# mLSTM cell and leaky-ReLU feed-forward: natural k of chunk 0 by transposing back, loads on other queues, another hand order of the first chunk

## The chip, the cores and the metric

The kernel runs on one core of one Trainium2 chip. The metric is device microseconds of one execution. A profile is one execution taken by the hardware profiler; its span runs from the first to the last instruction, and its own time is a little longer than the span.

The engines are TensorE (PE; its weight loads, PEld, are shown apart), VectorE (DVE), ScalarE (ACT), GpSimd (POOL) and SyncE (SP). SP and ACT both issue DMA transfers, each on a queue of its own; "SPq" and "ACTq" in the trace are such issues.

## The reference

Inputs are q, k, v and o_gate of shape (4 batches, 8 heads, 768 steps, 40), i_gate and f_gate of (4, 8, 768), and two weight matrices. The weights arrive as 64-bit floats.

```python
for t in range(S):
    m_new = np.maximum(f_gate[:, :, t] + m, i_gate[:, :, t])
    f_stab = np.exp(f_gate[:, :, t] + m - m_new)
    i_stab = np.exp(i_gate[:, :, t] - m_new)
    m = m_new
    C = f_stab * C + i_stab * einsum('bhd,bhe->bhde', vt, kt)
    n = f_stab * n + i_stab * kt
    h_tilde = einsum('bhde,bhe->bhd', C, qt)
    denom = np.maximum(np.abs(einsum('bhd,bhd->bh', n, qt)), 1.0)
    y[:, :, t] = sigmoid(o_gate[:, :, t]) * h_tilde / denom
x = y.transpose(0, 2, 1, 3).reshape(B * S, H * D)      # 3072 x 320
h = x @ w_in                                           # w_in 320 x 2048
out = np.maximum(0.01 * h, h) @ w_out                  # w_out 2048 x 320
```

## The kernel before

**Tiling.** Time is cut into six chunks of 128 steps. A step number s stands for one chunk and one batch: s = 4c + b. Within a chunk the recurrence is done in parallel form: scores of k against q, weighted by the gates, times v, plus the state that the chunk inherits. Chunk 0 inherits none, so it has code of its own. After a chunk of the cell come its feed-forward units, which `ff_units` returns as a list of small functions; the cell of chunk c and the feed-forward of chunk c-1 are interleaved.

**Who sets the order.** PE, DVE, ACT and POOL run in the order in which the program writes their instructions (`tc.manual_schedule`, line 1223). SP is not in that list: its issues are ordered by the framework. The DMA issues that the program gives to ACT stand in ACT's written order. Tiles in PSUM come from two rings of four buffers: tag "c" for the cell, tag "mm" for the feed-forward and the decay matrices.

**The first chunk** is `first_chunk` (line 1137), whose order is written out by hand. For each batch s from 0 to 3:

- `load` brings k and q (eight tokens of a head to a row) and v. `load_k` (391) brings k a second time, with a token on each partition ("natural"), 160 KB, into a slice of `rb_t`. `load_o` (396) brings the output gate, on ACT's queue.
- `u_transpose` (590) makes kqT, with the head dimension on the partitions, by matmuls against the identity, and copies it out of PSUM with an engine given to it: DVE for batches 0 and 1, ACT for 2 and 3.
- `spread_first` and `first_exp` (457, 486) make the decay matrix w of two batches at a time on PE, and its exponentials on ACT.
- `u_scores` (606) multiplies k and q and, on DVE, the decay matrix. `u_values` (690) multiplies by v, and `denominators` follows on DVE. `prep_o` is the tanh of the output gate on ACT. `gate` (698) makes x on DVE and POOL.
- `u_x` (786) transposes x on PE and copies it to xT with five ACT copies.
- `prep_vu` (508) scales v by the gates on POOL. `u_state` (680) multiplies natural k by it (`state`, 619) and copies the result into the state (`state_copy`, 630; two copies a batch, on DVE).

`narrow_weights` (244) turns a piece of the 64-bit weights into 32-bit in seven steps, an Abs on ACT and six on DVE; it is a generator, so the written order can put other work between two steps. `w_in` has four pieces, the first of which the feed-forward's units ffs[0] to ffs[3] need, the second ffs[4] to ffs[7]. ffs[0] and ffs[1] read x of batches 0 and 1, ffs[2] and ffs[3] of batches 2 and 3.

`gates(1)` (280) runs the scans of chunk 1 on DVE, `gates_exp(1)` (313) the exponentials on ACT, and writes a to the DRAM tensor `a_dr` (324). `spread` (438) reads it back, broadcast over partitions, as w of a step of chunk 1. `u_gates(1)` transposes the gates on PE and copies them with DVE.

After `first_chunk` the loads of chunk 1 are written (`feed`, 1115: v and the spread of w), and the main loop begins with ffs[2]; ahead of it in PE's order stands the first `u_split` (572) of chunk 1.

Of the kernel before, what the change touches and what calls it, by code (L numbers as in the profile page):

```python
# [19 lines left out]
def kernel(  # L20
# [28 lines left out]
    P = 128  # L49
# [41 lines left out]

    def load_fi(c):
        t = fi[c] = wk.tile([BH, 2, P], F32, name="fi")
        eng = nc.scalar if c < 3 else nc.sync
        eng.dma_start(t[:, 0, :], f_all[:, ts(c, P)])
        eng.dma_start(t[:, 1, :], i_all[:, ts(c, P)])

# [111 lines left out]
    def load_weights(n):  # L209

        m = n - QN
        if n < QN:
            dst = w_in[:, n, :]
        else:
            dst = w_out[:, 2 * m : 2 * m + 2, :].rearrange("p a d -> p (a d)")
        to = dst
        if wide:
            if n < 2:
                at = NF * GT - 2 * WC * (n + 1)
                raw = acts_l[:, at : at + 2 * WC].bitcast(U64)  # L220
            elif n < QN:
                raw = raw_t[:, WC * (n - 2) : WC * (n - 1)]
            elif m < 2:
                raw = w_out[:].rearrange("p f d -> p (f d)")[:, (2 + m) * WC : (3 + m) * WC].bitcast(U64)
            else:
                at = (4, 0, 1, 2, 3, 4)[m - 2] * HW
                raw = raw_t[:, at : at + HW]
            raws[n] = (raw, dst)
            to = raw
        if n < QN:  # L230
            src = moe_w_in[:, n * QC : (n + 1) * QC].rearrange("(k p) (r c) -> r p k c", p=DP, r=2)
            at = [0, 0]
# [80 lines left out]
    def gates_exp(c):  # L313
        bu, a, na = bus[c]
        if c == 0:
            nc.scalar.activation(bu[:, 1, :], i0[:BH], AF.Exp, bias=a[:BH, P - 1 :], scale=1.0)
            return
        for u in range(2):
            at = ts(u, SL)
            last = SL * (u + 1) - 1  # L320
            nc.scalar.activation(bu[:, 2, at], a[:, at], AF.Exp, bias=na[:] if u else 0.0, scale=1.0)
            nc.scalar.activation(bu[:, 1, at], bu[:, 0, at], AF.Exp, bias=a[:, last : last + 1], scale=1.0)
        if c > 0:
            nc.sync.dma_start(a_dr[c, 0].rearrange("u n t -> n u t"), a[:].rearrange("n (u t) -> n u t", u=2))
# [33 lines left out]
    def load(s):  # L358
        c, b = divmod(s, B)
        rows = ts(c, P)  # L360
        d = st.setdefault(s, {})
        n = s % NL
        d.update(k=kn[:, n], q=qn[:, n])
        if c == 0:
            d["va"] = S_t[n][:, 1]
            for t, src in ((kn, k), (qn, q)):
                nc.sync.dma_start(  # L367
                    t[:, n].rearrange("p h d -> p (h d)")[:, : TJ * D], src[b, :, rows, :].rearrange("h (g j) d -> h g (j d)", j=TJ),
                )
# [18 lines left out]
        if s < B + 2:  # L388
            load_late(s, 1)

    def load_k(s):
        to = rb_t[s % NR][:, 0, s // NR * Dm : (s // NR + 1) * Dm].rearrange("p (h d) -> p h d", d=D)
        nc.sync.dma_start(to, k[s, :, :P, :].rearrange("h p d -> p h d"))
        st[s]["k"] = to

    def load_o(s):
        c, b = divmod(s, B)
        at = NF * GT - 4 * WC - (s + 1) * Dm
        st.setdefault(s, {})["o"] = acts_l[:, at : at + Dm]
        nc.scalar.dma_start(  # L400
            st[s]["o"].rearrange("p (h d) -> p h d", d=D), o_gate[b, :, ts(c, P), :].rearrange("h p d -> p h d"),
        )

# [31 lines left out]

        return blocks(rb_t[s % NR][:, i, QW : QW + RL])[:, :, :w]

    def spread(s):

        c, b = divmod(s, B)  # L440
        d = st[s]
        w = wk.tile([P, H, P], F32, name="w", bufs=NL)
        d["w"] = w[:].rearrange("p h t -> p (h t)")[:, : H * SL].rearrange("p (h t) -> p h t", t=SL)
        for u in range(2):
            nc.sync.dma_start(d["w"][ts(u, SL)], a_dr[c, 0, u, b * H : (b + 1) * H, :].partition_broadcast(SL))

    def spread_q(s):

# [157 lines left out]
    def u_scores(s):  # L606
# [9 lines left out]
        for r in range(2):  # L616
            nc.vector.tensor_tensor(w[:, r::2, :], w[:, r::2, :], sc[r][:], op=ALU.mult)

    def state(s):
        c, b = divmod(s, B)  # L620
        d = st[s]
        dC = d["dC"] = psc.tile([P, PR, 2, V1], F32, name="dC", tag="c")
        for h in range(H):
            rows = slice(DP * (h % 2), DP * (h % 2) + D)
            nc.tensor.matmul(
                dC[rows, h // 2].rearrange("p k d -> p (k d)"), lhsT=d["k"][:, h, :D],
                rhs=d["vu"][:, h].rearrange("p k d -> p (k d)"), start=True, stop=True,
            )

    def state_copy(s):  # L630
        for r in range(2):
            rows = slice(DP * r, DP * r + D)
            nc.vector.tensor_copy(S_v[s % NL][SL : SL + D, 0, r::2, :, :V1], st[s]["dC"][rows])

    def state_of(s, u):

# [477 lines left out]

    def feed(s):
        load(s)
        spread(s)

    def feed_slowly(s):

# [16 lines left out]
    def first_chunk():  # L1137

        for n in range(2):
            load(n)  # L1140
        load_o(0)
        load_o(1)
        load_fi(1)
        load_weights(0)
        for n in range(2, B):
            load(n)
        load_weights(1)
        for n in range(B):
            load_k(n)
# [8 lines left out]
        u_transpose(1, nc.vector.tensor_copy)  # L1158
        load_kq(B)
        load_kq(B + 1)  # L1160
        load_weights(2)
        u_scores(0)
        u_scores(1)
        prep_o(0)
        prep_o(1)
        w = narrow_weights(0)
        next(w, None)
        load_o(2)
        load_o(3)
        load_fi(2)  # L1170
        ab = spread_first(a, 2)
        first_exp(ab, 2)
        prepare_tiles()
        next(w, None)
        next(w, None)
        u_values(0)
        gate(0)
        u_values(1)
        gate(1)
        prep_vu(0)  # L1180
        prep_vu(1)
        prepare_step(0)
        prepare_step(1)
        u_transpose(2, nc.scalar.copy)
        u_transpose(3, nc.scalar.copy)
        u_x(0)
        u_x(1)
        for _ in w:
            pass
        ffs = ff_units(0)  # L1190
        u_scores(2)
        u_scores(3)
        gates(1)
        gates_exp(1)
        ffs[0]()
        w = narrow_weights(1)
        next(w, None)
        prep_o(2)
        prep_o(3)
        next(w, None)  # L1200
        u_values(2)
        gate(2)
        next(w, None)
        u_values(3)
        gate(3)
        ffs[1]()
        u_x(2)
        for _ in w:
            pass
        u_x(3)  # L1210
        u_state(0)
        u_state(1)
        prep_vu(2)
        prep_vu(3)
        u_gates(1)
        u_state(2)
        u_state(3)
        prepare_step(2)
        prepare_step(3)
        return ffs  # L1220
# [123 lines left out]
```

## Time and profile before

| | |
|---|---|
| median of 3 runs | 514.63 us (513.19 to 515.49) |
| the profiled execution, its own time | 512.01 us |
| its span | 510.2 us |
| mean granted TensorE clock | 0.983 |
| PE busy | 493.4 us, 97% of the span |
| DVE, ACT, POOL busy | 338.6, 172.9, 144.2 us |
| DMA moved | 59.90 MB |

The page cuts the span into 40 slices of 12.8 us and gives, for each, the busy share of an engine in tenths (9 is 90% or more), the granted clock of TensorE in tenths, and the busy share of the DMA engines. A row of the timeline reads: start, duration, engine, line, operation, output<-input, shape, count, and in brackets the idle time ahead of it with what ended it. A row of the waits reads: the engine and line that waited, the one waited for, then microseconds in total, how often, and the longest.

### The profile page before, as it was taken

To read this page: it belongs to the slowest core of one execution; us is meant where nothing else is said; L and a number is where in the kernel's file an instruction comes from. 1 tells how busy PE (TensorE), PEld (TensorE's weight loads), DVE (VectorE), ACT (ScalarE), POOL (GpSimd) and SP (SyncE) were. 2 spreads that over 40 slices of the span, in tenths; PEclk is the share of its full clock that TensorE was granted. 3 is DMA by queue.
4 is the path that set the end of the run, shared out by engine and by line. 5 is a ranking of instruction groups with operands and counts; after the bars stand their busy time and mean duration, and the time that the engine had idled before them with its cause. 6 is when DMAs were issued, how large, how long until landed. Compare 5 with 4: busy or idle time off the path is not lost.

```text
span 510.2 us, 13235 instructions
## 1 busy us (share of the span) xinstructions
PE 493.4 (97%) x5346; PEld 384.4 (75%) x5346; DVE 338.6 (66%) x553; ACT 172.9 (34%) x462; POOL 144.2 (28%) x177
## 2 busy tenths in 40 slices
PE   8959798999999999999999999999999999999997
PEld 6848687867755469965479965489955489999997
DVE  4556999899973976924976734866623767864831
ACT  3163666752452331042421143511322510035210
POOL 3161725424320501620502701403700302200011
PEclk9878899999999999999999999999999999999999
DMA  6999886886460584872684772784861211200001
GB/s 140 184 161 174 175 221 152 217 159 149 90 165 9 114 165 120 151 155 90 138 164 122 144 163 77 156 155 111 167 176 33 58 53 39 89 5 1 1 1 51
DMA packets 161836, 59.90 MB, mean 117 GB/s; under 512 B 124336, under 2 KB 152560, under 8 KB 161776
## 3 DMA queue, kind: packets, MB, share of 16 engines
q1 hardware_dynamic: 117488, 51.20, 44.0%
q10 hardware_dynamic: 44288, 7.87, 9.6%
q8 instruction: 42, 0.69, 0.6%
q14 instruction: 18, 0.15, 0.1%
HBM read 52.33 MB, written 6.70 MB: 116 GB/s over the span
## 4 chain that ended last, share of the span: by engine, by line
PE 83%; SPq 5%; DMA 5%; DVE 2%; ACT 2%; POOL 2%; issue 1%; POOLq 0%; ACTq 0%; DVEq 0%
PE ph L813 32%; PE po L891 30%; PE pq L998 6%; PE po L848 6%; PE pT L748 3%; PE sd L667 3%; DMA acts<-in_moe_w_in_dram 2%; SPq L367 1%; DMA qn<-in_q_dram 1%; SPq L235 1%; PE sd L672 1%; DMA raw<-in_moe_w_in_dram 1%; PE tk L582 1%; PE hN L718 1%; SPq L414 1%
## 5 line engine op out<-in xcount | busy, mean ns | idle before, releaser
L813 PE MATMUL ph<-xT,w_in 64*128 64x512 f32 (+1 forms) x960 | 180.3, 527 | 0.0
L813 PEld LDWEIGHTS ph<-xT,w_in 64*128 64x128 f32 x960 | 92.5, 190 | 73.9 <-issue 68.0
L891 PEld LDWEIGHTS po<-w_out,acts 128*128 128x128 f32 x640 | 87.3, 190 | 3.4 <-issue 3.0
L891 PE MATMUL po<-w_out,acts 128*128 128x160 f32 x640 | 89.1, 300 | 0.0
L821 ACT ACTIVATE acts<-ph 128x512 f32<-128x512 f32 (+1 forms) x96 | 45.1, 522 | 119.7 <-PE ph L813 107.0
L645 POOL TENSOR_TENSOR S<-S,f 40x336 f32<-40x336 f32 x36 | 31.1, 863 | 130.9 <-PE pT L748 96.0
L677 DVE TENSOR_TENSOR qn<-w,sd 64x512 f32<-64x512 f32 x40 | 27.4, 684 | 41.5 <-PE sd L672 28.9
L506 ACT ACTIVATE w<-w,gT 128x64 f32<-128x64 f32 x160 | 41.2, 337 | 22.7 <-DMA S<-in_v_dram 11.2
L891 PE MATMUL po<-raw,acts 128*128 128x160 f32 x320 | 44.7, 300 | 0.0
L891 PEld LDWEIGHTS po<-raw,acts 128*128 128x128 f32 x320 | 43.6, 190 | 0.3
L848 PE MATMUL po<-w_out,acts 128*128 128x320 f32 x128 | 36.5, 437 | 0.0
L498 POOL TENSOR_TENSOR w<-w,i 128x512 f32<-128x512 f32 x20 | 28.4, 1429 | 24.4 <-DMA w<-a_dr 14.6
L762 POOL TENSOR_TENSOR xb<-xb,den 128x320 f32<-128x320 f32 x16 | 11.6, 727 | 76.9 <-DVE xb L759 76.9
L755 DVE STREAM_TRANSPOSE hb<-pT 128x512 f32<-128x512 f32 x16 | 11.4, 713 | 31.0 <-PE pT L748 30.8
L848 PEld LDWEIGHTS po<-w_out,acts 128*128 128x128 f32 x128 | 23.6, 190 | 9.3 <-issue 0.3
L559 DVE TENSOR_TENSOR qn<-kqT,ea 64x512 f32<-64x512 f32 x32 | 27.5, 860 | 1.0
L926 POOL TENSOR_TENSOR y<-y,raw 128x160 f32<-128x160 f32 x10 | 8.9, 894 | 64.2 <-ACT y L925 64.2
L667 PEld LDWEIGHTS sd<-kqT 40*64 40x64 f32 x640 | 20.0, 135 | 6.1 <-issue 6.1
L766 DVE STREAM_TRANSPOSE x<-xb 128x512 f32<-128x512 f32 x16 | 18.0, 1128 | 7.7 <-POOL xb L762 7.7
L891 PE MATMUL po<-raw 128*128 128x160 f32 x160 | 22.5, 299 | 0.0
L891 PEld LDWEIGHTS po<-raw 128*128 128x128 f32 x160 | 22.0, 190 | 0.0
L667 PE MATMUL sd<-kqT 40*64 40x64 f32 x640 | 21.6, 220 | 0.0
(185 smaller groups left out, 698.4 us busy)
## 6 DMA issues: line engine op xcount, KB each, us to landing
rb<-in_k_dram SPq DMA_DIRECT2D x64, 80.0 KB
rb<-in_q_dram SPq DMA_DIRECT2D x64, 80.0 KB
rb<-in_o_gate_dram SPq DMA_DIRECT2D x64, 80.0 KB
ea<-a_dr SPq DMA_DIRECT2D x32, 128.0 KB
raw<-in_moe_w_out_dram SPq DMA_DIRECT2D x6, 640.0 KB
w<-a_dr ACTq DMA_DIRECT2D x24, 128.0 KB
xT<-x_dr SPq DMA_DIRECT2D x32, 96.0 KB
x_dr<-x SPq DMA_DIRECT2D x64, 40.0 KB
```

Source lines behind the costliest of these rows:

```text
L498: nc.gpsimd.tensor_tensor(w, w, cm2.unsqueeze(1).to_broadcast([P, H, SL]), op=ALU.add)
L506: yield nc.scalar.activation(w[:, h, :], w[:, h, :], AF.Exp, bias=gT[c][:, 0, bh : bh + 1], scale=1.0)
L559: nc.vector.tensor_tensor(mixed(s)[rows, 1 - r], d["kqT"][rows, 1].rearrange("p (h t) -> p h t", t=SL), d["ea"][rows], op=ALU.mult,)
L645: nc.gpsimd.tensor_tensor(new, old, g, op=ALU.mult)
L667: nc.tensor.matmul(bank[1 - u][toks, h, :], lhsT=kqT[rows, 0, ts(h, SL)], rhs=kqT[rows, 1, ts(h, SL)], start=True, stop=True,)
L677: nc.vector.tensor_tensor(mixed(s)[toks, u], w[toks], bank[1 - u][toks], op=ALU.mult)
L766: nc.vector.transpose(in_blocks(xq[:]), xb[:].rearrange("p (j n) d -> p j n d", n=TB))
L813: nc.tensor.matmul(ph[r][:, cols], lhsT=w_row(r, slot, j), rhs=xT[DP * r : DP * (r + 1), slot, cols], start=(slot == 0), stop=(slot == KC ...
L821: nc.scalar.activation(acts[:, f, cols], ph[r][:, cols], AF.Prelu, alpha=0.01)
L848: nc.tensor.matmul(po[n][:], lhsT=acts[:, f, ts(n, P)], rhs=w_out[:, f, :], start=(f == 0), stop=(f == NF - 1),)
L891: nc.tensor.matmul(bank[:], lhsT=left[:, f, :], rhs=right[:, f, :], start=f == 0, stop=f == KH - 1)
L998: nc.tensor.matmul(bank[r][:, e, :], lhsT=left(r)[rows, e], rhs=right(r)[rows], start=n == 0, stop=n == len(terms) - 1,)
```

## The change

- `load_k` is removed. A new `u_natural` makes natural k of chunk 0 by transposing kqT back on PE, four 128x128 transposes per batch, with one ACT copy into the same place.
- The o loads of batches 2 and 3 are issued by SP, right after the loads of q, k and v; those of batches 0 and 1 stay on ACT. The f and i gates of chunk 2 are issued by SP.
- The write of a to `a_dr` for chunk 1 is issued by ACT, and so are the spreads of w for the first two steps of chunk 1 (4 and 5), which now stand in `first_chunk`.
- The two copies of kqT of batch 1 and all state copies of chunk 0 run on ACT.
- The hand order of `first_chunk` is another. Loads of k and q of step 5 stand behind w_in's third piece.

```diff
     def load_fi(c):
-        eng = nc.scalar if c < 3 else nc.sync
+        eng = nc.scalar if c < 2 else nc.sync
...
         if c > 0:
-            nc.sync.dma_start(a_dr[c, 0].rearrange("u n t -> n u t"), a[:].rearrange("n (u t) -> n u t", u=2))
+            eng = nc.scalar if c == 1 else nc.sync
+            eng.dma_start(a_dr[c, 0].rearrange("u n t -> n u t"), a[:].rearrange("n (u t) -> n u t", u=2))
...
-    def load_k(s):
-        to = rb_t[s % NR][:, 0, s // NR * Dm : (s // NR + 1) * Dm].rearrange("p (h d) -> p h d", d=D)
-        nc.sync.dma_start(to, k[s, :, :P, :].rearrange("h p d -> p h d"))
-        st[s]["k"] = to
-
-    def load_o(s):
+    def load_o(s, eng):
...
-        nc.scalar.dma_start(
+        eng.dma_start(
...
-    def spread(s):
+    def spread(s, eng):
...
-            nc.sync.dma_start(d["w"][ts(u, SL)], a_dr[c, 0, u, b * H : (b + 1) * H, :].partition_broadcast(SL))
+            eng.dma_start(d["w"][ts(u, SL)], a_dr[c, 0, u, b * H : (b + 1) * H, :].partition_broadcast(SL))
...
+    def u_natural(s):
+
+        nk = psc.tile([P, PR, P], F32, name="nk", tag="c")
+        for j in range(PR):
+            nc.tensor.transpose(nk[:, j], st[s]["kqT"][:, 0, ts(j, P)], ident[:])
+        to = rb_t[s % NR][:, 0, s // NR * Dm : (s // NR + 1) * Dm].rearrange("p (h d) -> p h d", d=D)
+        nc.scalar.copy(to, nk[:].rearrange("p j (r d) -> p (j r) d", r=2)[:, :, :D])
+        st[s]["k"] = to
...
     def state_copy(s):
...
-            nc.vector.tensor_copy(S_v[s % NL][SL : SL + D, 0, r::2, :, :V1], st[s]["dC"][rows])
+            nc.scalar.copy(S_v[s % NL][SL : SL + D, 0, r::2, :, :V1], st[s]["dC"][rows])
...
     def feed(s):
         load(s)
-        spread(s)
+        if "w" not in st[s]:
+            spread(s, nc.sync)
```

The body of `first_chunk` after the change, from the loads on:

```python
load(0); load(1); load_o(0, nc.scalar); load_o(1, nc.scalar); load_fi(1)
load_weights(0); load(2); load(3); load_o(2, nc.sync); load_o(3, nc.sync); load_weights(1)
gates(0); gates_exp(0); warm(9); ab = spread_first(a, 0); gates_T(0, bu); first_exp(ab, 0)
u_transpose(0, nc.vector.tensor_copy); u_transpose(1, nc.scalar.copy)
prep_vu(0); prep_vu(1)
load_kq(B); load_fi(2); load_weights(2); load_kq(B + 1)
u_scores(0); ab = spread_first(a, 2); u_scores(1)
prep_o(0); prep_o(1); u_natural(0); u_natural(1)
u_values(0); gate(0); u_values(1); gate(1)
first_exp(ab, 2); prepare_tiles()
w = narrow_weights(0); next(w, None)
u_x(0); u_x(1)
u_transpose(2, nc.scalar.copy); u_transpose(3, nc.scalar.copy)
for _ in w: pass
ffs = ff_units(0)
u_state(0); u_state(1); prepare_step(0); prepare_step(1)
u_scores(2); ffs[0](); u_scores(3)
u_values(2); prep_o(2); gate(2); u_values(3); prep_o(3); gate(3)
gates(1); gates_exp(1); ffs[1]()
w = narrow_weights(1); next(w, None); next(w, None)
u_x(2); u_x(3); prep_vu(2); prep_vu(3)
for _ in w: pass
u_gates(1)
for n in (B, B + 1): st[n] = {}; spread(n, nc.scalar)
u_natural(2); u_state(2); u_natural(3); u_state(3)
prepare_step(2); prepare_step(3)
```

More of the change, by code (lines that the diff above doesn't have):

```diff
@@ L1140, in first_chunk @@
             load(n)
-        load_o(0)
-        load_o(1)
+        load_o(0, nc.scalar)
+        load_o(1, nc.scalar)
         load_fi(1)
@@ L1146, in first_chunk @@
             load(n)
+        load_o(2, nc.sync)
+        load_o(3, nc.sync)
         load_weights(1)
-        for n in range(B):
-            load_k(n)
         gates(0)
@@ L1157, in first_chunk @@
         u_transpose(0, nc.vector.tensor_copy)
-        u_transpose(1, nc.vector.tensor_copy)
+        u_transpose(1, nc.scalar.copy)
+        prep_vu(0)
+        prep_vu(1)
         load_kq(B)
+        load_fi(2)
+        load_weights(2)
         load_kq(B + 1)
-        load_weights(2)
         u_scores(0)
+        ab = spread_first(a, 2)
         u_scores(1)
@@ L1165, in first_chunk @@
         prep_o(1)
[L1166 to L1175, printed above, removed]
+        u_natural(0)
+        u_natural(1)
         u_values(0)
@@ L1179, in first_chunk @@
         gate(1)
[L1180 to L1183, printed above, removed]
+        first_exp(ab, 2)
+        prepare_tiles()
+        w = narrow_weights(0)
+        next(w, None)
+        u_x(0)
+        u_x(1)
         u_transpose(2, nc.scalar.copy)
         u_transpose(3, nc.scalar.copy)
-        u_x(0)
-        u_x(1)
         for _ in w:
@@ L1190, in first_chunk @@
         ffs = ff_units(0)
+        u_state(0)
+        u_state(1)
+        prepare_step(0)
+        prepare_step(1)
         u_scores(2)
+        ffs[0]()
         u_scores(3)
+        u_values(2)
+        prep_o(2)
+        gate(2)
+        u_values(3)
+        prep_o(3)
+        gate(3)
         gates(1)
         gates_exp(1)
-        ffs[0]()
+        ffs[1]()
         w = narrow_weights(1)
[L1197 to L1206, printed above, removed]
+        for _ in range(2):
+            next(w, None)
         u_x(2)
+        u_x(3)
+        prep_vu(2)
+        prep_vu(3)
         for _ in w:
             pass
[L1210 to L1214, printed above, removed]
         u_gates(1)
+        for n in (B, B + 1):
+            st[n] = {}
+            spread(n, nc.scalar)
+        u_natural(2)
         u_state(2)
+        u_natural(3)
         u_state(3)
```

## The prediction

> **What bounds the kernel now.** I read the page's slices first, then the windows by stage, and then only the stage that is not full of TensorE work.
>
> ```profile
> PE   8959798999999999999999999999999999999997
> PEclk9878899999999999999999999999999999999999
> DMA  6999886886460584872684772784861211200001
> ```
>
> From the sixth slice on TensorE is busy and at full clock. The holes and the low clock lie in the first 60 us, and there the transfers are dense. The windows say it in microseconds (columns: length, then busy time of PE, weight loads, DVE, ACT, POOL; granted clock, DMA share, GB/s).
>
> ```profile
> 30.00:36.00 6.00, 2.85 (x10) 1.74 (x12) 1.32 (x1) 5.99 (x13) 4.06 (x8) 0.75 0.96 134
> 54.00:60.00 6.00, 3.89 (x98) 3.33 (x100) 5.74 (x13) 2.03 (x3) 4.65 (x11) 0.74 0.90 175
> 60.00:140.00 80.00, 78.00 (x1106) 62.39 (x1103) 74.75 (x108) 45.96 (x125) 33.00 (x30) 1.00 0.72 163
> 140.00:500.00 360.00, 360.00 (x3514) 274.47 (x3513) 225.52 (x367) 102.62 (x282) 86.69 (x101) 1.00 0.45 100
> ```
>
> After 60 us TensorE has 2.0 us of idle in 440. So the time of the whole kernel is the moment at which TensorE reaches the third feed-forward unit, ffs[2], plus a tail that the diff does not touch. In the trace that moment is 59.46. Every microsecond by which it moves is a microsecond of the kernel.
>
> What holds it up before that? The waits of the first 60 us, and the timeline of ScalarE and TensorE:
>
> ```profile
> PE xt L795 <- ACT kqT L604: 4.9, 1, 4.9
> PE dC L625 <- POOL vu L520: 2.5, 2, 2.2
> ACT w L491 <- DMA acts<-in_o_gate_dram: 7.8, 1, 7.8
> SPq L393 <- DMA acts<-in_moe_w_in_dram: 9.0, 3, 5.8
> ```
>
> ```profile
> 22.09 2.70 ACTq L400 DMA_DIRECT2D acts<-in_o_gate_dram  x2
> 26.20 2.82 ACTq L95 DMA_DIRECT2D fi<-in_f_gate_dram  x1
> 29.07 0.43 ACTq L96 DMA_DIRECT2D fi<-in_i_gate_dram  x1
> 29.55 2.32 ACT L491 ACTIVATE w<-ab 128x256 f32<-128x256 f32 x8 [7.79 <-DMA acts<-in_o_gate_dram]
> 31.67 3.93 ACT L604 COPY kqT<-tkq 128x512 f32<-128x512 f32 x4
> ...
> 32.98 0.66 PE L795 MATMUL xt<-ident,x 128*128 128x128 f32 x2 [4.88 <-ACT kqT L604]
> ...
> 50.24 0.44 PE L795 MATMUL xt<-ident,x 128*128 128x128 f32 x2
> 50.52 0.27 PE L796 MATMUL xt<-ident,x 128*64 128x128 f32 x1
> ...
> 59.46 2.79 PE L813 MATMUL ph<-xT,w_in 64*128 64x256 f32 x20
> ```
>
> ScalarE computes nothing from 21.75 to 29.55: it stands at four DMA issues. Behind them wait its exponentials, the copies of the transposes, and so TensorE.
>
> **How an issue waits.** The trace's completion records (the last of the 16 increments of a transfer's semaphore) explain those issues. The second o load goes out at 24.39; the transfer eight places ahead of it, counted over both queues together, completed at 24.37. The f load goes out at 26.20, after one that completed at 26.18. The k loads go out at 29.67, 31.26 and 33.62, after w_in pieces that completed at 29.65, 31.24 and 33.60. None of these issues needs the data it waited for. In this kernel an issue needs a place that the transfer eight ahead has given up, whichever engine issued either of them, and an engine that reaches it early stands still.
>
> **The change, part by part.** I rebuilt the order of the four engines by hand up to ffs[2], each instruction at its traced duration, each started when its engine, its inputs and its PSUM buffer (four in rotation) are free. Done so for the kernel before, the sum puts ffs[2] at 60.0 against 59.46 in the trace; 0.6 comes off the new sum too.
>
> 1. *The four loads of natural k (L393) go.* Nothing waits for them: they complete at 36.36 to 38.98, and their first reader runs at 52.0. What they free is the stream: 640 KB, about 0.9 us per load by the spacing of these completions, 3.5 us in all for everything behind.
>
> 2. *In their place 16 transposes and four copies.* A 128x128 transpose costs 0.14 us at full clock (L795 at 50.24, its follower 0.28 later, two of them) and 0.22 at half (32.98). So 2.2 to 3.6 us on TensorE: 1.2 ahead of values(0), on the path, the rest in a hole. A copy of 128x320 from PSUM is not in the trace; L798 takes 0.37 for 128x256, L542 0.46 for 128x320 from SBUF. I take 0.44, four times, on ScalarE.
>
> 3. *The o and f/i issues go to SyncE.* ScalarE is free at 21.75 instead of 29.50: 7.8 us. On SP they queue ahead of w_in(1), which completes at 35.3 and is not read before 44.8: that costs nothing unless SP falls 9 us behind.
>
> 4. *More on ScalarE.* The two copies of kqT(1) fall into idle time at 12 to 15. Eight state copies come over from DVE (0.33 each there; 64-row copies on ScalarE are 0.26 to 0.37, I take 0.31: 2.5 us). The first exponentials of batches 2 and 3 stand ahead of the Abs of w_in(0), which ends at 24.2 instead of 21.75; DVE's six steps on it end at 32.9.
>
> 5. *The hand order.* From there: u_x(1) 27.6, its five copies until 29.4 (1.64), four kqT copies at 0.98 until 33.3, scores(2) 34.5, ffs[0] until 36.8 (2.3; before it ran at 40.30 to 44.2), scores(3) 1.2 and two times values at 1.85 until 41.7, ffs[1] until 43.9 (before 50.2). DVE: gate(3) 42.7, gates(1) 1.7, exponentials 1.0: 45.4. So far the change gains 6 us.
>
> 6. *What is left stands in one row on ScalarE.* From 45.4: the issue of a_dr 0.5, Prelu 0.6, Abs of w_in(1) 1.4, ten copies of xT 3.3, four spread issues at 0.57 = 2.3, copy of natural k(2) 0.45, state(2) on TensorE 0.5, its copy 0.6, natural k(3) 0.45, state(3) 0.5, u_split 1.1. TensorE, done with u_gates at 46.3, waits for this row about 8 us. ffs[2]: 57.4, less 0.6 = 56.8. Four of the six microseconds are lost again, and without any DMA wait the change gains **2.7 us**.
>
> 7. *The wait.* a_dr now stands in ScalarE's row. SyncE's order is not written by hand, and before, a_dr went out late:
>
> ```profile
> 50.99 0.54 SPq L324 DMA_DIRECT2D a_dr<-a  x1
> 55.67 1.13 SPq L445 DMA_DIRECT2D w<-a_dr  x2
> ```
>
> Its data was ready at 43.2; four v loads, an o load and two pieces of w_in(3) went first, and the transfer eight ahead completed at 50.05. On SyncE that cost nothing. On ScalarE everything in point 6 is behind it, and DVE's steps on w_in(1) after the Abs. Bounds: with the same neighbours, the eighth ahead is now the q load of batch 5 (it has moved behind w_in(2)); by the stream 3.5 us earlier it completes near 47.0, a wait of 1.6. Were a_dr put behind all that SyncE can issue without chunk 1's gates, it would be a v load of batch 5 (61.49 before; less 3.5, less 1.5 for the spreads that no longer stand ahead): 56.5, a wait of 11.1. Below that, nothing: 0. In the order of before a_dr was already placed 7 us of transfers behind its data; now the hand order puts the gates behind ffs[0], both values and both gates, while SyncE's list is four loads shorter, so its place moves back, not forward. I take 52, the middle: a wait of **6.6 us**. The four spreads then find their places free.
>
> Sum: -2.7 + 6.6 = +3.9. It is made on the profiled execution (512.01, span 510.2) and carried to the median: 514.63 + 3.9 = **518.5**.
>
> Two rules of the Trainium skill, beside the rows. "DMA: Bandwidth & Descriptors", section "Issuing engines are not separate DMA queues", says that the issuing engine changes nothing but the sequencer's issue time. By it alone a_dr and the spreads would cost ScalarE their 2.8 us of issue and no wait, 511.9; the issues at 24.39 and 26.20 show a wait besides. "TensorE: Matmul & The Clock Gate", Part 4, gives some 275 ns for a 128x128 transpose in a kernel and says that transposes don't count as activity for the clock; an estimate from it is 4.4 us instead of 2.2 to 3.6, and a stretch at half clock after natural(0) and (1), up to 1.7 us. The rows at 50.24 speak against the first; for the second no row here has transposes alone.
>
> **Rivals.** *No wait (chance 0.24).* a_dr finds its place free because SyncE is far behind in issuing. For it: from 36 to 45 SP's issues follow each other at 0.6 us without waiting. Against: all four ScalarE issues in the dense stretch waited or were long. Time 514.6 - 2.7 = 511.9; if the 1.3 us of waits behind POOL at 82 to 84 go too, 510.6. *A small wait eats the gain (0.26).* Between 0.2 and 5 us, the lower bound above among it: 512.1 to 517; at a wait of 2.7, 514.6. That the removed loads were hidden anyway belongs here: by themselves they give nothing. *The wait decides (0.50).* From 5.3 us of wait the kernel is slower by over 0.5%, up to 11.1 - 2.7 = +8.4: 523.0.
>
> **Numbers.** About 0.5% (2.6 us) is what a measurement of this kernel can tell from no change. The forecast is the third case, 518.5, its own range 517.2 to 523.0. The range over all is 510.6 to 523.0: from the gain without waits to the longest wait. Faster 0.24, same 0.26, slower 0.50, the cases as they stand.
>
> **What would show it.** In the changed profile: L491 for batches 2 and 3 near 21 and ffs[0] near 34.5 (points 3 to 5); a TensorE hole ahead of L625 for batch 2, ended by the natural copy; ScalarE idle ahead of L324's issue, with the wait put to a load it does not read. If that issue follows the exponentials within 1 us, the forecast is wrong and the first rival right. If ffs[0] isn't there before 38, my order by hand is wrong.

## The result and the profile after

The changed kernel takes 523.16 us (median of 4 runs, 522.65 to 523.75), the kernel before 515.06 on the same chip: ratio 1.016, interval 1.0125 to 1.0196. It is slower by 8.1 us. The forecast was slower by 3.9, with 523.0 as the upper end of its range.

The profiled execution of the changed kernel took 523.52 us, its span is 521.7: 11.5 us more than the span of before. The medians differ by less, because the profiled execution of before, 512.01, lies 3.0 below the median of its runs. Moments below are from the profiles, gains and losses from the medians.

The page's slices of the changed kernel (13 us each) show where it went:

```profile
PE   7887079999999999999999999999999999999997
PEclk9978579999999999999999999999999999999999
DMA  7899975854344086595295674484871311200001
```

The fifth slice, 52 to 65 us, holds no TensorE work at all; before, it was seven tenths full. The windows put it in microseconds (columns as before: length, busy PE, weight loads, DVE, ACT, POOL, granted clock, DMA share, GB/s):

```profile
48.00:54.00 6.00, 2.10 (x10) 1.63 (x10) 0.00 (x0) 0.33 (x2) 1.42 (x4) 0.56 1.07 223
54.00:60.00 6.00, 0.00 (x0) 0.00 (x0) 2.73 (x3) 4.63 (x12) 0.00 (x0) 0.50 0.95 261
60.00:66.00 6.00, 0.00 (x0) 0.00 (x0) 4.53 (x6) 0.40 (x2) 0.00 (x0) 0.50 1.13 223
60.00:140.00 80.00, 70.61 (x1156) 57.95 (x1157) 65.10 (x96) 44.20 (x113) 28.29 (x26) 0.92 0.61 134
```

In the first of these windows ScalarE and VectorE stand nearly still as well, in the third ScalarE; the transfers alone are dense throughout. From 60 to 140 TensorE is busy for 70.61 us (78.00 before); 8.4 of the 9.4 us that it is idle lie before 72.7. The timeline of the changed kernel (start, length, engine, line; a "q" marks the issue of a transfer) names the instructions:

```profile
47.28 0.26 ACT L321 ACTIVATE bu<-a 32x64 f32<-32x64 f32 x1 [7.26 <-DVE a L295]
54.89 0.34 ACTq L325 DMA_DIRECT2D a_dr<-a  x1
55.27 0.66 ACT L826 ACTIVATE acts<-ph 128x256 f32<-128x256 f32 x2 [6.95 <-DMA raw<-in_moe_w_in_dram]
61.25 5.89 ACTq L441 DMA_DIRECT2D w<-a_dr  x4
67.19 0.43 ACT L621 COPY rb<-nk 128x320 f32<-128x320 f32 x1 [6.78 <-DMA w<-a_dr]
67.75 0.79 PE L630 MATMUL dC<-vu,rb 128*40 128x42 f32 x16 [17.28 <-ACT rb L621]
72.71 2.65 PE L818 MATMUL ph<-xT,w_in 64*128 64x256 f32 x22
```

Read it from the bottom. ffs[2] starts at 72.71; before, at 59.46. TensorE had waited 17.28 us for the copy of natural k of batch 2. That copy stood behind four spreads on ScalarE, whose issues took from 61.25 to 67.14. These stood behind ten copies and the Abs, and those behind the write of a_dr, which went out at 54.89, though its data was there at 47.3 (VectorE's L295) and ScalarE was through the exponentials ahead of it at 48.3. The releaser in brackets at L826, a piece of w_in, is nothing that the Prelu reads: it is the transfer whose place the write took.

The completion records of the semaphores, read as in the prediction, confirm each wait:

| issue on ScalarE | goes out | the transfer eight ahead is complete |
|---|---|---|
| write of a_dr | 54.89 | 54.868 (a piece of w_in(3)) |
| spread 1 | 61.25 | 61.232 (w_out) |
| spread 2 | 63.16 | 63.135 (w_out) |
| spread 3 | 65.31 | 65.289 (a v load) |
| spread 4 | 66.69 | 66.669 (a v load) |

All five went out within 0.03 us of the completion of a transfer they have nothing to do with. What a "place" is can be read from the issues' records: in every run the transfers that SyncE and ScalarE issue share eight semaphores, handed out in turn, and an issue goes out after the transfer before it on its own semaphore has completed.

### The profile page after: what moved, and what is told of

Its sections match the earlier page's. It is cut to its first block, busy times and chain, and to the rows that moved or that the text cites. A ratio compares the mean times of both kernels' runs of the same rounds, so it can differ in the third digit from the quotient of the medians.

```text
span 521.7 us, 13262 instructions
## 1 busy us (share of the span) xinstructions
PE 491.7 (94%) x5362; PEld 384.0 (74%) x5362; DVE 330.2 (63%) x543; ACT 179.4 (34%) x476; POOL 138.4 (27%) x177
## 4 chain that ended last, share of the span: by engine, by line
PE 79%; SPq 7%; DMA 5%; DVE 4%; ACT 2%; POOL 1%; issue 1%; ACTq 0%; POOLq 0%
PE po L896 30%; PE ph L818 29%; PE pq L1003 6%; PE po L853 5%; PE pT L753 3%; DMA S<-in_v_dram 3%; PE sd L672 3%; SPq L377 3%; SPq L235 2%; DMA w<-a_dr 1%; DMA qn<-in_q_dram 1%; SPq L410 1%; PE sd L677 1%; SPq L95 1%; DVE raw L269 1%
## 5 line engine op out<-in xcount | busy, mean ns | idle before, releaser
L818 PE MATMUL ph<-xT,w_in 64*128 64x512 f32 (+1 forms) x960 | 178.5, 523 | 0.0
L818 PEld LDWEIGHTS ph<-xT,w_in 64*128 64x128 f32 x960 | 91.2, 187 | 73.1 <-issue 67.9
L826 ACT ACTIVATE acts<-ph 128x512 f32<-128x512 f32 (+1 forms) x96 | 45.2, 522 | 126.6 <-PE ph L818 106.8
L760 DVE STREAM_TRANSPOSE hb<-pT 128x512 f32<-128x512 f32 x16 | 11.5, 717 | 30.9 <-PE pT L753 30.8
```

Source lines behind the costliest of these rows:

```text
L818: nc.tensor.matmul(ph[r][:, cols], lhsT=w_row(r, slot, j), rhs=xT[DP * r : DP * (r + 1), slot, cols], start=(slot == 0), stop=(slot == KC ...
L826: nc.scalar.activation(acts[:, f, cols], ph[r][:, cols], AF.Prelu, alpha=0.01)
```

## The experiments

Each run stands beside runs of the kernel before on its own chip (medians 513.4 to 515.1); ratios are to those, and 0.1% is 0.5 us. Two variants from different chips are better compared by their ratios than by their medians. "ffs[2]" is its start in the run's profile.

### Where the five issues of the gates stand

**All five on SyncE, the rest of the change kept.**

```diff
-            eng = nc.scalar if c == 1 else nc.sync
-            eng.dma_start(a_dr[c, 0] ...)
+            nc.sync.dma_start(a_dr[c, 0] ...)
...
-        for n in (B, B + 1): st[n] = {}; spread(n, nc.scalar)
```

> The changed kernel with chunk 1's write of a to a_dr and the four spreads of steps 4 and 5 issued by SyncE again, as before; all else of the change stays. Theory (ScalarE stands at DMA issues that need a place given up by a transfer eight ahead): the 6.6 us at the write and the 4.5 us between the spreads go, and the spreads' own 2.3 us too; ffs[2] comes at 57 to 60 instead of 72.7, 509 to 513 us. Rival (the new hand order and the copies moved to ScalarE cost the time; the DMA waits only fill a hole that is there anyway): ffs[2] stays above 66, 519 us or more.

Measured: 517.31 us, ratio 1.0069 (1.005 to 1.0088); ffs[2] at 58.80. The theory of the wait is right for ffs[2], which comes 13.9 us earlier, and the time was wrong: only 5.9 us of that arrive (4.7 by the ratios). The timeline of this run shows what took the rest:

```profile
67.37 0.82 ACT L501 ACTIVATE w<-w,gT 128x64 f32<-128x64 f32 x3 [5.89 <-POOL w L493]
...
68.65 4.68 PE L817 MATMUL ph<-xT,w_in 64*128 64x256 f32 x20 [5.03 <-ACT acts L825]
```

There is a second gate. The exponentials of step 4 (L501) stand ahead of the Prelus of ffs[2] on ScalarE. They need GpSimd's mask of w, and w needs the spreads, which land at 64.2 to 66.8. So the third unit waits 5.03 us. Behind that hole it runs almost wholly at half clock (until 72.98), 4.68 us for 20 matmuls where the two units ahead took 4.82 for 40: some 2.3 us more. Together that is 7.3 of the 8.0 us that did not arrive. It is not enough to reach ffs[2] early; w of step 4 must arrive as well.

**Only the write, or only the spreads, on SyncE**: one of the two edits above alone.

> Only the write to a_dr goes back to SyncE; the four spreads stay on ScalarE. Theory: the wait of 6.6 us at the write goes, the spreads then wait for the write, which SyncE issues in its own order, and for their places; ffs[2] at 63 to 69, 514 to 520 us, between the changed kernel and the one with both on SyncE. If the spreads' waits are nothing of their own, 509 to 513. Rival (the hand order): 521 to 524, as with the whole change.

Measured: 523.16 us, ratio 1.0192 (1.0165 to 1.0219), no gain; ffs[2] at 70.75. On SyncE the write went out at 55.17, no earlier, and completed at 60.77. The timeline:

```profile
60.84 4.26 ACTq L440 DMA_DIRECT2D w<-a_dr  x4
...
65.15 0.43 ACT L620 COPY rb<-nk 128x320 f32<-128x320 f32 x1 [12.31 <-DMA w<-a_dr]
```

ScalarE now is through its copies at 52.8, stands at the first spread until the write has landed, and then at the other three: 12.31 us in all. The wait has moved from one issue to the next one in the row.

> The changed kernel with the four spreads issued from SyncE, the write of a_dr still from ScalarE. My theory: of the two delays on ScalarE, the write's (6.6 us) stays and the spreads' row (61.25 to 67.14) goes; the copy of natural k of batch 2 then follows the last copy of xT near 60.5 instead of 67.19, ffs[2] comes at 65.5 to 66.5 instead of 72.71, and the time is 516 to 519 (not the whole 6 us less, since the weights w of step 4 land no earlier and hold the units behind ffs[2]). Rival: only both moves together gain, as moving the write alone gave nothing (ffs[2] 70.75, 523.16); then 521 to 524.

Measured: 518.87 us, ratio 1.011 (1.0083 to 1.0138); ffs[2] at 65.46. As the theory said: the copy of natural k ran at 59.86, right behind the copies of xT. The row of spreads on ScalarE is worth 7.2 us of ffs[2], 4.3 us by the medians and 2.6 by the ratios. With all five on SyncE, 1.6 more are gained.

**The same five issues put on ScalarE in the kernel before**, nothing else changed:

```diff
-            nc.sync.dma_start(a_dr[c, 0] ...)
+            eng = nc.scalar if c == 1 else nc.sync
+            eng.dma_start(a_dr[c, 0] ...)
...
         u_gates(1)
+        for n in (B, B + 1): st[n] = st.get(n, {}); spread(n, nc.scalar)
         u_state(2)
```

> The kernel before with the other part alone: chunk 1's write to a_dr and the spreads of steps 4 and 5 are issued by ScalarE, at the places where the change puts them. Theory: the write reaches ScalarE at 44 and waits there for 3 to 7 us, the spreads wait again; ffs[2] 5 to 11 us later, 519 to 526 us. Rival (the hand order): 514 to 517.

Measured: 518.53 us, ratio 1.0085 (1.0069 to 1.01). The part alone costs 4.6 us; ffs[2] at 65.52. Its write went out at 49.89, 0.02 after the transfer eight ahead was complete. Its four spreads, from 58.62 to 61.4, did not wait: their places had been free for 0.85 us or more.

**All five kept on ScalarE, but later in its order.** First the four spreads behind the states of batches 2 and 3, then the write too, behind the state of batch 2:

```diff
+        u_natural(2); u_state(2); u_natural(3); u_state(3)
         for n in (B, B + 1): st[n] = {}; spread(n, nc.scalar)
-        u_natural(2); u_state(2); u_natural(3); u_state(3)
```

> The changed kernel with ScalarE's four spreads behind the two natural copies and the two states instead of ahead of them; the write of a_dr stays where it is. Theory: the spreads' waits cost through what stands behind them, the natural copies; with these ahead, the copy of batch 2 follows the copies of xT near 60.8, ffs[2] comes near 66 instead of 72.71; the spreads go some 3 us later, so that the weights w of step 4 land near 70 and the third unit's Prelu waits for them: a part is given back, 518 to 521. Rival: the later landing takes all of it back, 522 to 524.5.

Measured: 523.83 us, ratio 1.0179 (1.0141 to 1.0217). ffs[2] came at 66.80, as the theory had it, and the rival had the time. Behind the second gate everything was lost again: 3.70 us of waiting, then a third unit at half clock (4.91 us where the two ahead took 5.06 together). The timeline:

```profile
66.80 5.06 PE L818 MATMUL ph<-xT,w_in 64*128 64x256 f32 x40
75.57 4.91 PE L818 MATMUL ph<-xT,w_in 64*128 64x256 f32 x20 [3.70 <-ACT acts L826]
```

```diff
         u_natural(2); u_state(2)
+        gates_write(1, nc.scalar)
         u_natural(3); u_state(3)
```

> The run before, and besides the write of a_dr put behind the state of batch 2 in ScalarE's order, not ahead of the Prelu of ffs[1]. All of the change is kept, its issues on ScalarE too; only the places of five issues in the row are others. Theory: the row from the gates' exponentials to the state of batch 2 runs without a stop (48.3 to some 56), the write finds a place that came free near 55 and waits at most 1 us, the spreads wait for the write's landing near 60 with little behind them; ffs[2] near 59.5 to 61.5, and the arrival of w of step 4 near 66 is then what holds the third unit: 514.5 to 518, as with all five issues on SyncE (517.31). Rival: the stops only move to the next things in the row (Abs of the third w_in and the copies of kqT of step 4) and ffs[2] comes no earlier than 65: 519 to 523.

Measured: 524.46 us, ratio 1.0191 (1.0156 to 1.0226); ffs[2] at 63.77, and then 4.76 us at the second gate. The theory was wrong: moved back in the order, the write did not find a free place, it waited longer. The timeline:

```profile
52.98 0.61 ACT L645 COPY S<-dC 40x168 f32<-40x168 f32 x2 [1.02 <-PE dC L637]
60.23 0.34 ACTq L317 DMA_DIRECT2D a_dr<-a  x1
60.60 0.43 ACT L628 COPY rb<-nk 128x320 f32<-128x320 f32 x1 [7.01 <-DMA w_out<-in_moe_w_out_dram]
```

ScalarE is ready for it at 53.6. Four places came free from 54.46 to 55.15, and issues of SyncE that are listed ahead of the write used those, from 55.52 to 59.50; the write waited for a piece of w_out that was issued only at 54.43 and completed at 60.203. "Eight ahead" is counted in the order in which the program lists the issues. An issue that is listed later gets a later place, even if its engine reaches it first.

### What making natural k costs

**Made instead of loaded in the kernel before**; the transposes of batches 0 and 1 ahead of their values, those of 2 and 3 between the scores:

```diff
-        for n in range(B): load_k(n)
...
+        u_natural(0); u_natural(1)
         u_values(0)
...
-        u_scores(2); u_scores(3)
+        u_scores(2); u_natural(2); u_scores(3); u_natural(3)
```

> The kernel before with one part of the change alone: natural k of chunk 0 is made by transposing back, the four loads are gone. By the predicted prices: 2.2 to 3.6 us of transposes and 1.8 us of copies, partly in holes, 514 to 518 us. Rival (the loads held up the stream, and with it the write to a_dr and the spreads, by 3.5 us): 510 to 513.

Measured: 518.16 us, ratio 1.007 (1.0048 to 1.0091); ffs[2] at 65.86, 6.4 later than before. The work is small, and it was sized rightly. The two first copies, though, stood behind the four issues on ScalarE, which here lasted until 31.7 (29.5 before). The timeline of this run:

```profile
30.64 1.06 ACTq L96 DMA_DIRECT2D fi<-in_i_gate_dram  x1
31.75 2.32 ACT L486 ACTIVATE w<-ab 128x256 f32<-128x256 f32 x8 [9.89 <-issue]
33.87 0.84 ACT L620 COPY rb<-nk 128x320 f32<-128x320 f32 x2
34.44 1.98 PE L596 MATMUL tkq<-ident,kn 128*64 128x64 f32 x32 [10.37 <-ACT rb L620]
```

TensorE waits 10.37 us, since the transposes of the next batch need the PSUM buffer that L620 empties.

**Loaded instead of made in the changed kernel**, once with the gates on SyncE, once with them on ScalarE:

```diff
+        for n in range(B): load_k(n)
...
-        u_natural(0); u_natural(1)
...
-        u_natural(2); u_state(2); u_natural(3); u_state(3)
+        u_state(2); u_state(3)
```

> The changed kernel with chunk 1's gates on SyncE (as in e1) and with natural k loaded again, so that the hand order, the o and f, i issues and the copies on ScalarE are what is left of the change. If making k costs time: faster than e1, 513 to 516 us. If the loads cost time in the stream: 518 to 522. If neither: 516 to 518.5, and the rest of e1's loss lies in the hand order.

Measured: 514.75 us, ratio 1.001 (0.9987 to 1.0033), 2.6 less than with k made (517.31).

> The changed kernel with natural k loaded by four transfers again instead of made by 16 transposes and four copies; the gates stay on ScalarE. Theory: the price of making k that the same edit showed with the gates on SyncE (2.6 us) comes off here too, 520 to 521.5, ffs[2] near 70. Rival, by point 1 of the prediction: the four loads are in the stream again, the write and the spreads wait 3.5 us longer for their places, and the time is 525 to 527.

Measured: 518.85 us, ratio 1.0103 (1.0079 to 1.0127), 4.3 less than the changed kernel; ffs[2] at 65.03. Two things differ here. No copy that TensorE's states need stands behind the spreads any more: the state of batch 2 ran at 53.51. And with four more transfers in the list the spreads have other transfers eight ahead of them, whose places had been free for 0.9 us or more: they went out from 59.85 to 62.4 without a wait, 2.5 us where the changed kernel took 5.9. So the 4.3 us are not the price of making k alone. By the ratios k loaded gains 0.6% in both places. The rival is refuted: the four loads pushed the write back by 0.5 us (55.41), not by 3.5. They did cost time further ahead: in the changed order the state of batch 0 comes early enough to wait 2.05 us for the loaded k, and ffs[0] starts at 38.77 instead of 36.28 (39.29 instead of 35.7 with the gates on SyncE).

### The issues that go to SyncE, and the second gate

**Only the o and f/i loads moved to SyncE, in the kernel before**, with the loads of step 5 behind w_in's third piece, as the change has them:

```diff
-        load_o(2); load_o(3); load_fi(2)
...
         load(0); load(1); load_weights(0); load(2); load(3)
+        load_o(2, nc.sync); load_o(3, nc.sync)
         load_weights(1)
...
-        load_kq(B); load_kq(B + 1); load_weights(2)
+        load_kq(B); load_fi(2); load_weights(2); load_kq(B + 1)
```

> The kernel before with one part of the change alone: o of batches 2 and 3 and f, i of chunk 2 are issued by SyncE. Theory: ScalarE is free at 21.75 instead of 29.5 and ffs[0] comes 4 to 7 us earlier; the gates of chunk 1 stay on SyncE, so nothing is paid back on ScalarE; 509 to 513 us. Rival (the transfers set the pace of this stage, and who issues them matters nothing): 514 to 516.

Measured: 510.69 us, ratio 0.9931 (0.9908 to 0.9955): faster than before. This is the part of the change that pays. ffs[2] came at 53.62, 5.8 earlier, and then the second gate held the third unit for 4.49 us, after which it took 4.01 us, most of it at half clock:

```profile
53.62 6.31 PE L813 MATMUL ph<-xT,w_in 64*128 64x256 f32 x40
64.42 4.01 PE L813 MATMUL ph<-xT,w_in 64*128 64x256 f32 x20 [4.49 <-ACT acts L821]
```

**The same, with the masks and exponentials of steps 4 and 5 two feed-forward units later**, so that the Prelus go first; then the same edit on the changed kernel with its gates on SyncE:

```diff
-        late = {}
+        late = {B: 3}
...
-                    if i == 0: prep_mask(B)
+                    if i == 1: prep_mask(B); prep_mask(B + 1)
```

> The kernel before with o of batches 2, 3 and f, i of chunk 2 issued by SyncE (as in e4), and the masks and exponentials of steps 4 and 5 moved behind two more feed-forward units, on POOL and ScalarE. Theory: in e4 TensorE stood 4.5 us because ScalarE waited for w of step 4 ahead of the Prelu of ffs[2], so the arrival of w (write to a_dr, then spread) is a second gate behind ffs[2]; with the exponentials behind, that wait goes: 505 to 508 us. Rival (the wait only moves to the scores of step 4, which need the same w): 510 to 512, as e4.

Measured: 509.95 us, ratio 0.9912 (0.9884 to 0.9941), the fastest of the study. The three units ran through from 52.90 without a stop, but TensorE loses time later instead, from 75.8 to 81.5, waiting for GpSimd and, from 78.7, at half clock: 0.7 us gained by the medians, which the intervals do not tell from nothing, as the rival had it.

> The changed kernel with chunk 1's gates on SyncE (as in e1) and the masks and exponentials of steps 4 and 5 moved behind two more feed-forward units. Theory of the second gate: the 5.0 us that TensorE stood behind the Prelu in e1 go, 511 to 514 us. Rival (what is left of the loss is work that the hand order and the copies on ScalarE added): 516 to 519.

Measured: 514.59 us, ratio 0.9999 (0.997 to 1.0029): 2.7 less than without the edit. It is the fastest form found that keeps the change's making of k and its hand order, and it equals the kernel before.

**Natural k made, on top of the fastest:** both edits above together.

> The kernel before with the loads of o and f/i on SyncE and the later masks (509.95), and natural k of chunk 0 made by transposing instead of loaded. Theory: the copies of natural k no longer stand behind the four issues on ScalarE, which in the kernel before cost 3.6 us with the same edit; what is left is the work itself, 1.2 us of transposes ahead of values(0) and 1.7 us of copies on ScalarE: 511 to 513. Rival: the 3.6 us are the work on TensorE at half clock and stay: 513.5 to 515. Third: the freed 3.5 us of the stream pay for it: 509 to 510.5.

Measured: 511.84 us, ratio 0.9955 (0.9933 to 0.9978): 1.9 us more than with k loaded, in line with the theory. With no issues ahead of its copies on ScalarE, making k costs less than the 3.6 us that it cost in the kernel before; it paid in none of the four places.

These runs also price what no run was made for, the new hand order with its copies on ScalarE. Two pairs differ in these alone: k made, the moved issues and the gates on SyncE, the exponentials late, 511.84 and 514.59 (ratios 0.9955 and 0.9999); k loaded, the same issues on SyncE, 510.69 and 514.75 (0.9931 and 1.001). The new order costs 0.4% and 0.8%, some 2 and 4 us; the intervals of the first pair just overlap, and the second has the wait for the loaded k in it. In the first pair ffs[2] comes 1.0 us later, 56.73 for 55.71, with VectorE's scans of chunk 1 at 42.51 instead of 36.73.

By the ratios the whole change can then be walked in four steps, each a run above: o and f/i issues to SyncE -0.7% (510.69), order and copies +0.8% (514.75), k made +0.6% (517.31), the five issues on ScalarE +0.9% (523.16), in all the 1.6% measured.

### The sizes: the clock, and the time of the data

**110, then 72, matmuls that nobody reads in TensorE's hole:**

```diff
         u_natural(2)
+        warm(110)
         u_state(2)
```

> The changed kernel with 110 matmuls of 128x128 whose result nobody reads, behind the transposes of natural k of batch 2, in the hole of TensorE from 50.5 to 67.75. Nothing else is changed. Theory: of the 13 us by which ffs[2] is late, some 2 us come from the clock, which is at half from 48.7 to 72.6: with it at full the 5.0 us from the copy of natural k to ffs[2] become 2.5 to 3.5, ffs[2] comes at 70.2 to 71.2 and the time is 520.5 to 522. Rival: in that stretch TensorE waits for copies on ScalarE and products on GpSimd, whose times don't hang on the clock; ffs[2] within 0.5 of 72.7, time 523 to 524.

Measured: 530.29 us, ratio 1.0341 (1.0301 to 1.0382). They took 24.7 us and ran past the hole, so the time says nothing; the clock's share can be read all the same. From the first matmul on the copy to ffs[2] it took 3.29 us (73.41 to 76.70) at full clock, and 4.96 in the changed kernel at half. The difference, 1.7, is an upper bound for the clock, as the late start also left GpSimd's products done.

> The changed kernel with 72 matmuls of 128x128 that nobody reads in TensorE's hole, behind the transposes of natural k of batch 2. 110 of them took 24.7 us, 0.225 each, and ran 4.3 us past the hole; 72 end near 65. Theory: with the clock up, the stretch from the first matmul on the copy of natural k to ffs[2] takes 3.3 us instead of 4.96, as it did in the run with 110; ffs[2] near 71.0 and the time 521 to 522. Rival: the matmuls' reads slow the other engines' work or the clock drops again before 67, and nothing is gained: 522.5 to 524.5.

Measured: 525.99 us, ratio 1.0224 (1.0193 to 1.0255). The matmuls ended at 66.4, TensorE then waited 2.72 us, and the clock was down again; ffs[2] came at 74.20. Windows of this run, of 1 us each:

```profile
68.00:69.00 1.00, 0.00 (x0) 0.00 (x0) 0.00 (x0) 0.40 (x1) 0.00 (x0) 1.00 0.84 186
69.00:70.00 1.00, 0.83 (x17) 0.78 (x18) 0.00 (x0) 0.02 (x1) 0.00 (x0) 0.60 1.09 215
75.00:76.00 1.00, 1.00 (x6) 0.81 (x6) 0.96 (x2) 0.98 (x3) 0.15 (x1) 0.50 0.54 158
76.00:77.00 1.00, 1.00 (x12) 0.85 (x10) 0.96 (x2) 0.99 (x3) 0.00 (x0) 0.99 0.67 151
```

The stretch took 5.03 us, nothing was gained. Why the run is 2.8 us slower than the changed kernel is not settled; its write went out 1.6 later (56.49).

**GpSimd's products for vu written behind the gates of chunk 1:**

```diff
-        prep_vu(2); prep_vu(3)
         for _ in w: pass
         u_gates(1)
+        prep_vu(2); prep_vu(3)
```

> The changed kernel with GpSimd's four products for vu of batches 2 and 3 behind the gates of chunk 1 instead of beside them, so that VectorE's steps on the gates run alone (0.41 and 0.28 us instead of 0.84 and 0.81). Theory: the gates' exponentials come about 1 us earlier, near 46.3, but the write of a_dr goes when a place comes free, not when its data is there: still within 0.5 of 54.9, ffs[2] within 0.7 of 72.7, time 522.5 to 524. Rival, by the prediction's own sum (a wait of 6.6 us behind the exponentials): a_dr near 53.9, ffs[2] near 71.7, time 521.5 to 522.2.

Measured: 525.16 us, ratio 1.0217 (1.0186 to 1.0248); ffs[2] at 72.53. The edit did not do what was meant: in GpSimd's own order the products stayed where they were, and its trace has them from 44.23 to 46.16, beside VectorE's steps from 44.39 to 46.07, which stayed at 0.84 and 0.80 us. The exponentials came 1.2 us earlier all the same (46.10), since the whole row before them did. The write went out at 55.91, a microsecond later than in the changed kernel, 0.02 after its place came free. Data that is earlier didn't make the write earlier; the theory's point holds, the rival's sum doesn't. Whether 2 us were lost is open: the profiled executions took 523.60 and 523.52, and the intervals overlap.

## Why the prediction was right in kind and wrong in size

| moment in the profile, us | before | predicted | after |
|---|---|---|---|
| ffs[0] starts | 40.30 | 34.5 | 36.28 |
| ffs[1] ends | 50.3 | 43.9 | 45.8 |
| gates' exponentials done | 44.2 | 45.4 | 48.3 |
| write of a_dr goes out | 50.99 | 52.0 | 54.89 |
| first spread goes out | | 57.8 | 61.25 |
| copy of natural k(2) | | 60.1 | 67.19 |
| ffs[2] starts | 59.46 | 63.4 | 72.71 |

(57.8 and 60.1 are point 6's row, counted on from 52.0.)

**Direction and mechanism: right.** The forecast was that the wait decides, with the rule that an issue needs the place of the transfer eight ahead. The five rows of the completion table and the pair with and without the five issues on ScalarE (523.16 and 517.31, or 0.9% by the ratios) show it. That the kernel came out slower rests on this only in part: without the five issues on ScalarE it is slower too, by 0.7%, which the forecast did not expect. By the Trainium skill, "DMA: Bandwidth & Descriptors", section "Issuing engines are not separate DMA queues", issuing from several engines saves only the sequencer's issue time, usually small. It does not speak of an issue that must first wait for a place; here such waits made the choice of the engine worth 5.9 us, and the measurement decides.

**Point 1** (the loads of k were hidden): in the kernel before, yes. That they free 3.5 us of the stream for everything behind is wrong: with them back in the changed kernel, ffs[0] starts 2.5 later, but the write only 0.5.

**Point 2** (work of making k): right. Eight transposes took 1.09 us at full clock, 0.14 each as taken; four at half took 1.12, 0.28 instead of 0.22; a copy 0.43 for 0.44. The rows at 50.24 do not speak against the 275 ns that the prediction quotes, though: a single transpose of these eight lasts 0.27 us. They start 0.11 apart and overlap, so such lengths can't be added up.

**Points 3 to 5** (hand order): the moments were right within 2 us up to ffs[1], and 2.9 late at the exponentials. ffs[0] is 1.8 late because the state copies of batches 0 and 1, 34.31 to 35.56, hold the scores of batch 2. VectorE's three steps L290, L293 and L295 add 1.4: 0.69, 0.84 and 0.81 us for 0.25, 0.41 and 0.28 in the kernel before.

**Point 6, a step that failed: "without any DMA wait the change gains 2.7 us".** With the five issues back on SyncE ffs[2] comes 0.7 us earlier than before (58.80 and 59.46), and the time is 3.3 us longer (517.31 and 513.97). So this term, taken as -2.7, measured about +3.3, although in this run ScalarE does not even bear the 2.8 us of issue that the row counts. What the five issues on ScalarE then add, 6.6 by the sum, measured 5.9, or 4.7 by the ratios. The terms of the row also add up to 57.1, not to 57.4.

**Point 7, the steps that failed.** In the changed kernel itself ffs[2] came 9.3 us later than the sum:

- *The write's place, "I take 52, the middle": 2.9 us.* The wait came out at 6.6, as sized, but by two errors that cancel. The data came 2.9 late, and the place came free at 54.87 instead of 52. In the run with vu written behind the gates the exponentials came 1.2 us earlier and the write 1.0 later: the place set the write, not the data's time.
- *"The four spreads then find their places free": 4.2 us, the largest error.* Each waited for its own place. From the write to the copy of natural k the row took 12.3 us instead of 8.1. The run with the spreads on SyncE shows it: there the copy came 5.6 us after the write went out (54.22 to 59.86).
- *From the copy to ffs[2], 5.5 us instead of 3.3.* Behind a hole of 17 us all of it ran at half clock; the sum had full clock. The run with 110 matmuls puts at most 1.7 of these 2.2 on the clock.

**"The time of the whole kernel is the moment at which TensorE reaches ffs[2], plus a tail that the diff does not touch."** For the changed kernel this held: span less ffs[2] is 450.7 before and 449.0 after; 449.6 and 449.6 with the write alone and the spreads alone on SyncE. It fails where ffs[2] is ready before w of step 4 is: 457.0 with all five on SyncE, 457.3 in the kernel before with o and f/i moved, 456.4 and 458.9 with the issues later on ScalarE. Most of the error of point 6 lies here: with all five on SyncE ffs[2] is 2.0 us later than its 56.8, but the tail is 6.3 us longer than before. The tail was taken as untouched, and the path through w of step 4, which ends behind ffs[2], was left out. The prediction's rival without waits, 511.9, promised more than removing the waits from ScalarE gives, 517.31.

**The other lines.** The signs named came: ScalarE idle ahead of the write's issue (L325 now), with the wait put to a load it does not read, and a hole of TensorE ended by the natural copy. The test that would have refuted the hand order (ffs[0] not before 38) did not strike.

## What to carry to other kernels

When an issue moves to another engine, find the transfer whose place it takes (in this program the one eight ahead in the order of the list) and when that one completes: the engine stops there, with everything behind it, and here putting the issue later in the list moved its place later too. Treat a chain of issues (a write, then the reads of it) as one unit: easing the write alone handed the wait to the spreads (523.16 both times). Before a gain is booked as "time of unit n", look for what else unit n+1 needs; here 8 of 13.9 us did not arrive, 7.3 of them through a second gate and the half clock behind its hole. And price each part of a change alone: only one of the four parts gained.

## What the hardware showed unexpectedly

The place of a transfer is fixed by the order of the list, not dealt out when an engine arrives: the write that was ready at 53.6 stood until 60.23 while four places came free by 55.15.

The clock fell to half at 69.19, 2.8 us after the last matmul, and came back to full at 76.02, 6.8 us after TensorE resumed, with a gap of 0.6 us in between (the run with 72 matmuls). In the trace's clock records the changes of this run lie at 41.89, 48.71, 69.19 and 76.02, and so 2, 6 and 2 times 3.41 us apart; in all the other runs, too, they are whole multiples of 3.41 us apart. The Trainium skill, "TensorE: Matmul & The Clock Gate", Part 1, gives free-running windows of some 3.4 us for both directions; this trace agrees. A fall 2.8 us after the last matmul is no contradiction, since the windows do not begin with it.

VectorE's three steps on the gates took 0.69, 0.84 and 0.81 us in every kernel with the changed hand order, and in each of these GpSimd's products (0.72 us) run beside them. With GpSimd idle they took 0.25, 0.41 and 0.28: in the kernels with the order of before, and in the changed kernel itself for chunk 2, at 76.58 to 77.59. So the slow steps go with GpSimd's work beside them; no run changed that alone.
